# Filling the first operand tile of split queries and keys with GpSimd copies instead of DMA moves

## The chip, the cores and the metric

One core of a Trainium2 chip runs the kernel. The metric is the device time of one execution in microseconds, the median of three runs. Engines are TensorE (PE in the profile, its weight loads PEld), VectorE (DVE), ScalarE (ACT), GpSimd (POOL) and SyncE (SP, here the queue that issues nearly all DMAs of the stage in question; `SPq` in a row is the issue of a DMA on it).

## The reference

Three parts follow one another; the change lies in the first, attention with a causal mask and a bias from cumulated sums:

```python
def _attn_ref(q, k, v, s):          # q, k, v: (4, 8, 576, 64) float32
    scores = scale * np.matmul(q, k.transpose(0, 1, 3, 2))
    cum = np.cumsum(np.maximum(s, 0.0), axis=-1)
    bias = -(cum[:, :, :, None] - cum[:, :, None, :])
    scores = np.where(causal, -1e9, scores + np.minimum(bias, 0.0))
    scores = scores - np.max(scores, axis=-1, keepdims=True)
    attn = np.exp(scores)
    attn = attn / (np.sum(attn, axis=-1, keepdims=True) + 1e-09)
    return np.matmul(attn, v)
...
x = _moe_ref(x=x, ...)              # 2304 tokens, 8 experts of capacity 288, 512 -> 1024 -> 512
return _moe2_ref(x=x, ...)          # 512 -> 2048 -> 512 for all tokens
```

## The kernel before, in words

The 32 heads of attention are worked off in 8 groups `g` of 4 heads, and each group in two pairs `pr` of 2 heads. A head takes 7 steps ("blocks") of the main loop, so a group takes `NB` = 28. The loop at the end of `attention` runs over the step number `t`; in each step it calls what was put into `todo` for this step, emits the scores of one block (`emit_s`), one or two jobs, and five blocks later the product with V (`emit_pv`). The order on every engine is the order in which this loop emits; there is no planner behind it. `later(n, fn)` puts a function n steps ahead, `job(early, due, fn)` puts one into a list that is worked off when there is time.

Float32 products are made of split operands: a number is a high part (`float32r`) and a low part, the difference. For q and k that works so. `load_qk` (L728 to L737) loads a pair in six DMAs into `qkraw[pr]`, the last of which (n = 5, L736) is the end of k, 64 rows of two heads. `t_unit` (L836) transposes with TensorE in three units: L844 for most of it, L849 for the last 64 rows of q and k, which thus waits for that last load. Behind each unit `evac` (L855, ScalarE) writes the high part into a buffer `qk` of four planes, and `low` (L860, VectorE) the low part. There are two such buffers, so a pair's ScalarE write waits until the moves out of the buffer two pairs before are done.

`dup` (L871) then spreads a pair over the operand tiles of the scores: `QKA[i]` (i = g mod 2; partitions 0 to 63 hold the high parts of q and k, further rows the bias, which L868 and L869 bring) and `QKB[i]` (low and high parts on 64 partitions each). Per pair that is six moves, two into `QKA` (n = 0, 1, one per head) at once and four into `QKB` (n = 2 to 5) some steps later. One moves 64 partitions x 1152 columns, 288 KB. A string says how each one is made: `a` by ScalarE, `v` by VectorE, `d` by a DMA of the SP queue. In steady groups all six are `d`. `guard` (L920) computes from `QKA` the row maxima, `m_row` writes them back (L961), and `emit_s` multiplies both tiles (L999, L1001).

Behind the scores ScalarE makes `P` = exp (L1008), ScalarE (L1011) or VectorE (L1015) its high part `Ph`, and GpSimd the low part `Pl` = P - Ph (L1016). GpSimd does this once per tile of scores, four times a head, in the order of widths 384, 384, 320, 512. Three products with V follow (L1036, L1037, L1038), of which the last reads `Pl`. Beside this VectorE reduces the maxima (L937) and, from step 75 on, prepares weights of the last part in three instructions per unit (L115, L118, L121).

On the SP queue all loads (`qkraw`, `vraw`, weights), all `d` moves, the bias rows, the maxima and the stores of results (L1071, L1074) stand in one line, in the order of emission.

Of the kernel before, what the change touches and what calls it, by code (L numbers as in the profile page):

```python
# [9 lines left out]
F32R = mybir.dt.float32r  # L10
# [10 lines left out]
B, H, S, D = 4, 8, 576, 64  # L21
# [9 lines left out]
def fb(ap):  # L31
    return ap.bitcast(F32)
# [677 lines left out]
def attention(ctx, tc, const, cv, q, k, v, s, w_gate, ident, L, x_dram, b_dram, setup):  # L710
    nc = tc.nc
# [105 lines left out]
    def later(n, fn, *args):  # L817
        todo.setdefault(now[0] + n, []).append((fn, args))
# [3 lines left out]
    def job(early, due, fn, *args):  # L822
        jobs.append((due, len(jobs), early, fn, args))
        jobs.sort()
# [11 lines left out]
    def t_unit(g, pr, n):  # L836

        if n == 0:
            QK[g, pr] = rot.tile([128, 4, S], F32R, name="qk", bufs=2)
        st = QK[g, pr]  # L840
        p = bank()
        if n < 2:
            for r in range(4):
                nc.tensor.transpose(p[:, 128 * r:128 * r + 128], qkraw[pr][:, n, r], ident)  # L844
            src, hd = p, st[:, 1 + n, 0:512]
            los = [(src, hd, st[:, 3 * (1 - n), 0:512])]
        else:
            for t in range(2):
                nc.tensor.transpose(p[:, 128 * t:128 * t + 128], qkraw[pr][:, t, 4], ident)  # L849
            src = p[:, :256].rearrange("p (t c) -> p t c", t=2)[:, :, :64]  # L850
            hd = st[:, 1:3, 512:]
            los = [(src[:, t], st[:, 1 + t, 512:], st[:, 3 * (1 - t), 512:]) for t in range(2)]

        def evac():
            nc.scalar.activation(hd, src, AF.Copy)  # L855
            later((1, 4)[pr] if g == 0 else 0, low)

        def low():
            for x, h, ld in los:
                nc.vector.tensor_sub(ld, x, fb(h))  # L860
        later(1, evac)
        if n == 2:
            later(max(2, NB * g + 14 * pr - 41 - now[0]) if g or pr == 0 else 2, dup, g, pr)

    def bias_rows(g, pr):
        i, hs = g % 2, slice(2 * pr, 2 * pr + 2)
        rows = b_dram[4 * g + 2 * pr:4 * g + 2 * pr + 2].rearrange("h j t -> j h t")
        nc.sync.dma_start(out=fb(QA[i])[66:68, hs, 64:], in_=rows[0:2])  # L868
        nc.sync.dma_start(out=fb(KA[i])[64:66, hs], in_=rows[2:4])  # L869

    def dup(g, pr):  # L871
        i = g % 2
        if g:
            bias_rows(g, pr)
        st = fb(QK[g, pr])
        moves = []
        for dst, r, t in ((fb(QKA[i])[0:64, :, 64:], 0, 1), (fb(QKB[i])[0:64], 0, 2), (fb(QKB[i])[64:128], 1, 0)):
            for e in range(2):
                moves.append((dst[:, 2 * pr + e], st[64 * e:64 * e + 64, t:t + 2].rearrange("p t c -> p (t c)")))

        def move(n):
            dst, src = moves[n]
            how = ('vvaaaa', 'adaddd')[pr][n] if g == 0 else 'dddvda'[n] if g == 1 else "d"
            if how == "a":
                nc.scalar.activation(dst.bitcast(F32R), src, AF.Copy)
            elif how == "v":
                nc.vector.tensor_copy(dst.bitcast(F32R), src)
            else:
                nc.sync.dma_start(out=dst, in_=src)
        for n in range(len(moves)):  # L890
            if n < 2:
                move(n)
            else:
                later(2 * n - 2 if g > 1 else (2, 4)[pr] + (0, 0, 2, 4, 3, 5)[n], move, n)
        units = GU if g else GU0
        for u in range(len(units)):
            at = u + 2 if g == 0 and pr else now[0] + {0: 1, 1: 5}.get(g, 8) + u
            job(at, max(at, NB * g + 14 * pr - 26 + 2 * u), guard, g, pr, u)
# [234 lines left out]
    t = -PRE  # L1133
    while t < len(blocks) or queue or jobs or any(k >= t for k in todo):
# [14 lines left out]
        if 7 - PRE <= t < 15 - PRE:  # L1149
            x, h = divmod(t - 7 + PRE, 4)  # L1150
# [49 lines left out]
```

## Time and profile before

| what | value |
|---|---|
| median of 3 runs | 1037.19 us (1036.14 to 1038.14) |
| the profiled execution's own time | 1036.92 us |
| its span, first to last instruction | 1035.2 us |
| mean granted clock of TensorE over the span | 0.978 |
| TensorE busy | 959.4 us (93%) |
| VectorE, ScalarE, GpSimd busy | 604.1, 632.3, 424.0 us |
| DMA moved | 105.57 MB in 133298 packets |

The first 290 us or so are attention, the rest the experts and the last part. In a row of instructions stand the start and the length in us, the engine, the line, the operation, what it writes and reads, and how many are merged; in brackets the idle time of the engine before it and what ended that. A row of waits gives the sum in us, the number of waits and the longest. Granted clock 1.00 is full speed.

### The profile page before, as it was taken

How to read it: one execution, taken by the hardware profiler on the slowest of the kernel's cores; microseconds unless marked ns; L12 is line 12 of the kernel's file. 1: busy time of each engine (PE TensorE's matmuls, PEld its weight loads, DVE VectorE, ACT ScalarE, POOL GpSimd, SP SyncE). 2: the span in 40 equal slices, each digit the busy share in tenths (PEclk: the TensorE clock that was granted, in tenths of full speed). 3: DMA queues.
4: the chain of work that ended last, by engine and by line, in shares of the span. 5: the costliest groups of instructions: out<-in, count | busy, mean ns of one | idle time of the engine just before them, and what ended most of it. 6: DMA issues, size and time to landing. Idle time of an engine off the chain costs nothing.

```text
span 1035.2 us, 21414 instructions
## 1 busy us (share of the span) xinstructions
PE 959.4 (93%) x7679; PEld 905.8 (88%) x7679; DVE 604.1 (58%) x1871; ACT 632.3 (61%) x1403; POOL 424.0 (41%) x429
## 2 busy tenths in 40 slices
PE   5889889988978789899999999999999999999996
PEld 4779878888846678899999999999999999999996
DVE  6767889889576667546444553644644554343343
ACT  7657767766944356536745754673674575575573
POOL 2546666666768622360351234126036024502401
PEclk8889999999999999999999999999999999999999
DMA  5798889894229323231230222213123022401200
GB/s 125 178 189 203 202 205 212 203 215 127 73 85 285 106 79 112 76 106 42 64 100 9 82 67 62 65 42 105 42 65 105 19 67 83 136 12 31 76 1 23
DMA packets 133298, 105.57 MB, mean 102 GB/s; under 512 B 63720, under 2 KB 114056, under 8 KB 133160
## 3 DMA queue, kind: packets, MB, share of 16 engines
q1 hardware_dynamic: 122520, 83.50, 32.0%
q10 hardware_dynamic: 7600, 11.27, 3.6%
q0 software_dynamic: 3072, 9.44, 3.0%
q8 instruction: 60, 0.98, 0.4%
q14 instruction: 46, 0.38, 0.1%
HBM read 69.55 MB, written 9.73 MB: 77 GB/s over the span
## 4 chain that ended last, share of the span: by engine, by line
PE 57%; issue 13%; DVE 12%; ACT 6%; POOL 6%; DMA 4%; SPq 1%; ACTq 0%; POOLq 0%; DVEq 0%
PE y L497 8%; PE y L498 7%; PE y L499 7%; PE hp L497 5%; PE hp L498 5%; PE hp L499 5%; PE words L497 3%; PE words L499 2%; PE words L498 2%; PE rt L298 2%; DVE junk L937 2%; DMA QKB<-qk 2%; POOL WI L92 1%; PE t L1081 1%; POOL WO L92 1%
## 5 line engine op out<-in xcount | busy, mean ns | idle before, releaser
L467 POOL TENSOR_TENSOR wt<-raw,wt 128x512 fp32r<-128x512 f32 x112 | 142.9, 1292 | 195.0 <-ACT wt L466 193.9
L1016 POOL TENSOR_TENSOR Pl<-P,Ph 128x384 fp32r<-128x384 f32 (+2 forms) x128 | 136.7, 1076 | 92.6 <-DVE Ph L1015 45.8
L497 PE MATMUL y<-act,WO 128*128 128x288 f32 x516 | 154.9, 300 | 3.2 <-ACT act L558 3.2
L498 PE MATMUL y<-act,WO 128*128 128x288 f32 x516 | 153.7, 298 | 0.2
L499 PE MATMUL y<-act,WO 128*128 128x288 f32 x516 | 152.7, 296 | 0.0
L497 PE MATMUL hp<-xu,WI 128*128 128x288 f32 x372 | 114.4, 307 | 7.8 <-DVE c L599 3.9
L498 PE MATMUL hp<-xu,WI 128*128 128x288 f32 x372 | 110.2, 296 | 0.4 <-DVE xu L535 0.2
L499 PE MATMUL hp<-xu,WI 128*128 128x288 f32 x372 | 110.0, 296 | 0.0
L497 PEld LDWEIGHTS y<-act,WO 128*128 128x128 f32 x516 | 97.8, 190 | 3.5 <-ACT act L558 3.4
L498 PEld LDWEIGHTS y<-act,WO 128*128 128x128 f32 x516 | 97.6, 189 | 0.9 <-DVE act L605 0.6
L499 PEld LDWEIGHTS y<-act,WO 128*128 128x128 f32 x516 | 97.5, 189 | 0.0
L466 ACT ACTIVATE wt<-raw 128x512 fp32r<-128x512 f32 x112 | 70.1, 626 | 41.3 <-PE y L499 17.1
L402 POOL DMA_INDIRECT xg<-x_dram,idx x24 | 22.6, 942 | 162.2 <-DVE rt L408 156.9
L599 DVE SCALAR_TENSOR_TENSOR hp<-c,hp 128x288 f32<-128x288 f32 x75 | 34.6, 461 | 87.6 <-ACT c L594 87.6
L591 ACT ACTIVATE c<-c 128x288 f32<-128x288 f32 x128 | 56.3, 440 | 44.8 <-DVE c L590 41.7
L1008 ACT ACTIVATE P<-s 128x384 f32<-128x384 f32 (+2 forms) x128 | 63.5, 503 | 30.6 <-PE s L1001 17.6
L497 PEld LDWEIGHTS hp<-xu,WI 128*128 128x128 f32 x372 | 70.5, 190 | 11.8 <-DVE c L599 5.6
L1036 PE MATMUL pv<-Ph,VH 128*128 128x320 f32 (+4 forms) x224 | 71.8, 320 | 1.5 <-DVE xT L1055 1.5
L498 PEld LDWEIGHTS hp<-xu,WI 128*128 128x128 f32 x372 | 70.4, 189 | 1.0 <-DVE xu L579 0.6
L999 PE MATMUL s<-QKB 128*128 128x320 f32 (+4 forms) x224 | 70.4, 314 | 0.8 <-DVE mx L937 0.8
L499 PEld LDWEIGHTS hp<-xu,WI 128*128 128x128 f32 x372 | 70.5, 190 | 0.0
L497 PE MATMUL y<-act,wt 128*128 128x288 f32 x224 | 69.1, 309 | 0.0
(287 smaller groups left out, 2939.1 us busy)
## 6 DMA issues: line engine op xcount, KB each, us to landing
raw<-in_moe_w_dram SPq DMA_DIRECT2D x120, 256.0 KB
QKB<-qk SPq DMA_DIRECT2D x55, 288.0 KB
QKA<-qk SPq DMA_DIRECT2D x29, 288.0 KB
qkraw<-in_q_dram SPq DMA_DIRECT2D x32, 128.0 KB
qkraw<-in_k_dram SPq DMA_DIRECT2D x32, 128.0 KB
vraw<-in_v_dram SPq DMA_DIRECT2D x32, 128.0 KB
x_dram<-xn SPq DMA_DIRECT2D x16, 256.0 KB
r<-in_moe_w_in_dram ACTq DMA_DIRECT2D x8, 512.0 KB
```

The costliest lines, as they stand in the source:

```text
L402: nc.gpsimd.indirect_dma_start(out=xg[:JW], out_offset=None, in_=x_dram, in_offset=bass.IndirectOffsetOnAxis(ap=idx[:JW, j:j + 1], axis=0))
L466: nc.scalar.activation(t[:, 0], r, AF.Copy)
L467: nc.gpsimd.tensor_sub(t[:, 1], r, fb(t)[:, 0])
L497: nc.tensor.matmul(out_ap, ah, bh, start=first, stop=False)
L498: nc.tensor.matmul(out_ap, ah, bl, start=False, stop=False)
L499: nc.tensor.matmul(out_ap, al, bh, start=False, stop=last)
L591: nc.scalar.activation(a, a, AF.Exp)
L599: nc.vector.scalar_tensor_tensor(u, a, 0.5, p[:, :CAP], op0=OP.subtract, op1=OP.mult)
L999: nc.tensor.matmul(p[:m, at:at + n], KB[i][:, h, kc], QB[i][:, h, q0:q1], start=ti in (1, 2) and j == 0, stop=False, skip_group_check=True)
L1008: nc.scalar.activation(P[:, :n], p[:, :n], AF.Exp, scale=0.125)
L1016: nc.gpsimd.tensor_sub(Pl[:, :n], P[:, :n], fb(Ph)[:, :n])
L1036: nc.tensor.matmul(o, VH[i][:, a, hs], ph, start=first, stop=False)
```

## The change

In every group but the first, the moves n = 0 and 1 (into `QKA`) are no longer DMAs. Each is made by two GpSimd copies of 64 partitions x 576 columns, one for q and one for k, so four copies in a row per pair. And the four later moves, in groups from the third on, are emitted at 1, 3, 5 and 7 steps behind `dup` instead of 2, 4, 6 and 8.

```diff
         def move(n):
             dst, src = moves[n]
-            how = ('vvaaaa', 'adaddd')[pr][n] if g == 0 else 'dddvda'[n] if g == 1 else "d"
-            if how == "a":
+            how = ('vvaaaa', 'adaddd')[pr][n] if g == 0 else 'ppdvda'[n] if g == 1 else 'ppdddd'[n]
+            if how == "p":
+                for t in range(2):
+                    x = slice(S * t, S * t + S)
+                    nc.gpsimd.tensor_copy(dst.bitcast(F32R)[:, x], src[:, x])
+            elif how == "a":
                 nc.scalar.activation(dst.bitcast(F32R), src, AF.Copy)
...
             if n < 2:
                 move(n)
             else:
-                later(2 * n - 2 if g > 1 else (2, 4)[pr] + (0, 0, 2, 4, 3, 5)[n], move, n)
+                later(2 * n - 3 if g > 1 else (2, 4)[pr] + (0, 0, 2, 4, 3, 5)[n], move, n)
```

Below are places where the order on an engine changes; line numbers behind L884 are 4 higher in the changed kernel. First the SP queue of before at the second pair of the fifth group (`QKA_102` and `QKB_104` are that group's operand tiles, `qkraw_89` the raw tile of the pair after it):

```order
L961 DMA QKA_103<-mt 1x5x128 x2
L78 DMA r_2065<-in_moe_w_out_dram 128x256
L868 DMA QKA_102<-b_dram 2x2x576
L869 DMA QKA_102<-b_dram 2x2x576
L889 DMA QKA_102<-qk 64x1152 x2
L736 DMA qkraw_89<-in_k_dram 64x2x64
L889 DMA QKB_104<-qk 64x1152 x2
L733 DMA qkraw_90<-in_q_dram 128x4x64
```

And the SP queue of the change at the same place:

```order
L965 DMA QKA_103<-mt 1x5x128 x2
L78 DMA r_2079<-in_moe_w_out_dram 128x256
L868 DMA QKA_102<-b_dram 2x2x576
L869 DMA QKA_102<-b_dram 2x2x576
L736 DMA qkraw_89<-in_k_dram 64x2x64
L893 DMA QKB_104<-qk 64x1152 x2
L733 DMA qkraw_90<-in_q_dram 128x4x64
```

The two `QKA` moves are gone from between the bias rows and the last load of k; nothing else has changed its place here.

GpSimd before, around the same `dup`:

```order
L1016 TENSOR_TENSOR Pl<-P,Ph 128x384 x2
L1016 TENSOR_TENSOR Pl<-P,Ph 128x320
L1016 TENSOR_TENSOR Pl<-P,Ph 128x512
L1016 TENSOR_TENSOR Pl<-P,Ph 128x384 x2
L1016 TENSOR_TENSOR Pl<-P,Ph 128x320
```

GpSimd in the change:

```order
L1020 TENSOR_TENSOR Pl<-P,Ph 128x384 x2
L1020 TENSOR_TENSOR Pl<-P,Ph 128x320
L1020 TENSOR_TENSOR Pl<-P,Ph 128x512
L887 CAST QKA_102<-qk 64x576 x4
L1020 TENSOR_TENSOR Pl<-P,Ph 128x384 x2
L1020 TENSOR_TENSOR Pl<-P,Ph 128x320
```

The four copies stand between the last difference of one head, 512 wide, and the first of the next, 384 wide.

The third place is the SP queue in the start, where the first pair of the third group begins. Before (`QKA_102` and `QKB_104` are the third group's, `QKB_105` the second's):

```order
L889 DMA QKB_105<-qk 64x1152
L868 DMA QKA_102<-b_dram 2x2x576
L869 DMA QKA_102<-b_dram 2x2x576
L889 DMA QKA_102<-qk 64x1152 x2
L889 DMA QKB_105<-qk 64x1152
L733 DMA qkraw_89<-in_k_dram 128x4x64
L889 DMA QKB_104<-qk 64x1152
```

In the change:

```order
L893 DMA QKB_105<-qk 64x1152
L868 DMA QKA_102<-b_dram 2x2x576
L869 DMA QKA_102<-b_dram 2x2x576
L893 DMA QKB_105<-qk 64x1152
L893 DMA QKB_104<-qk 64x1152
L733 DMA qkraw_89<-in_k_dram 128x4x64
```

The last move of the second group has no `QKA` moves ahead of it any more, and the first `QKB` move of the third group now follows it directly, ahead of a load of k.

## Rows read from the trace of the kernel before

**Rows 1.** The page, parts 1 and 2: busy us, and tenths in 40 slices of the span

```profile
PE 959.4 (93%) x7679; PEld 905.8 (88%) x7679; DVE 604.1 (58%) x1871; ACT 632.3 (61%) x1403; POOL 424.0 (41%) x429
...
PEclk8889999999999999999999999999999999999999
DMA  5798889894229323231230222213123022401200
```

**Rows 2.** Busy time by stretch: window, length, engines (instructions), clock, DMA share, GB/s

```profile
22.00:68.00 46.00, 35.76 (x210) 32.13 (x211) 29.26 (x103) 27.62 (x54) 23.13 (x22) 0.76 0.87 185
68.00:156.00 88.00, 81.11 (x600) 74.80 (x600) 70.89 (x247) 62.43 (x141) 54.40 (x49) 0.98 0.86 198
156.00:235.00 79.00, 71.70 (x533) 64.67 (x531) 70.03 (x238) 57.18 (x128) 50.05 (x55) 1.00 0.90 210
```

**Rows 3.** Waits of TensorE, 68 to 235 us: sum, times, longest

```profile
PE t L849 <- DMA qkraw<-in_k_dram: 10.0, 7, 3.2
PE t L931 <- DVE mx L937: 1.5, 4, 0.5
```

**Rows 4.** Instructions in order of time on SP's queue, 135.6 to 137 us

```profile
135.67 1.18 SPq L889 DMA_DIRECT2D QKA<-qk  x2
136.90 0.99 SPq L736 DMA_DIRECT2D qkraw<-in_k_dram  x1
```

**Rows 5.** Instructions in order of time on TensorE, at 142.03 us

```profile
142.03 0.33 PE L849 MATMUL t<-ident,qkraw 128*128 128x128 f32 x1 [3.18 <-DMA qkraw<-in_k_dram]
```

**Rows 6.** Waits of TensorE, 22 to 68 us

```profile
PE t L849 <- issue: 3.2, 1, 3.2
PE t L931 <- DVE qk L860: 3.2, 1, 3.2
```

**Rows 7.** Waits of ScalarE, 22 to 68 us

```profile
ACT qk L855 <- DMA QKB<-qk: 6.6, 2, 3.9
```

**Rows 8.** The chain of waits, 40 to 66 us: start, length, what

```profile
44.11 3.55 DMA QKB<-qk
...
56.46 4.88 DMA QKB<-qk
```

**Rows 9.** Instructions in order of time on SP's queue, 35 to 36 and 55 us

```profile
35.30 1.11 SPq L889 DMA_DIRECT2D QKA<-qk  x2
...
55.07 1.29 SPq L889 DMA_DIRECT2D QKA<-qk  x2
```

**Rows 10.** Busy time by stretch, as rows 2, behind three long waits

```profile
48.00:54.00 6.00, 4.64 (x18) 3.93 (x19) 5.49 (x14) 2.83 (x7) 2.81 (x3) 0.50 0.88 175
62.00:68.00 6.00, 5.18 (x21) 4.84 (x22) 3.62 (x13) 2.56 (x7) 1.47 (x2) 0.50 1.17 205
143.00:147.00 4.00, 4.00 (x23) 4.00 (x21) 4.00 (x9) 1.60 (x5) 3.30 (x3) 0.57 1.06 250
```

**Rows 11.** The page, part 6: DMA issues, KB of one

```profile
QKA<-qk SPq DMA_DIRECT2D x29, 288.0 KB
```

**Rows 12.** Groups of instructions on GpSimd to 290 us: busy us, mean ns, idle before

```profile
L1016 POOL TENSOR_TENSOR Pl<-P,Ph 128x384 fp32r<-128x384 f32 x64 | 67.5, 1057 | 62.6 <-DVE Ph L1015 43.2 <-ACT Ph L1011 8.6 <-PE t L931 5.4
L1016 POOL TENSOR_TENSOR Pl<-P,Ph 128x512 fp32r<-128x512 f32 x32 | 41.8, 1307 | 21.7 <-ACT qk L855 9.1 <-ACT Ph L1011 5.6 <-PE t L931 5.5
...
L800 POOL TENSOR_SCALAR_AFFINE_SELECT band<-band 128x576 f32<-128x576 f32 x1 | 0.8, 763 | 0.1
...
L804 POOL COPY idwg<-ident 128x128 f32<-128x128 f32 x1 | 0.3, 287 | 0.0
```

**Rows 13.** Instructions in order of time on GpSimd, 201.4 to 204.5 us

```profile
201.52 1.28 POOL L1016 TENSOR_TENSOR Pl<-P,Ph 128x512 fp32r<-128x512 f32 x1 [1.08 <-ACT Ph L1011]
203.35 1.01 POOL L1016 TENSOR_TENSOR Pl<-P,Ph 128x384 fp32r<-128x384 f32 x1 [0.56 <-ACT Ph L1011]
```

**Rows 14.** Instructions in order of time on TensorE, at 206.14 us

```profile
206.14 0.28 PE L1038 MATMUL pv<-Pl,VH 128*128 128x256 f32 x1
```

**Rows 15.** Two lines of VectorE, 60 to 260 us: duration in ns, min/median/max

```profile
L1015 DVE CAST Ph<-P x48: 311/360/1002, 64.0 to 254.5; 128x384 fp32r<-128x384 f32 x24, 128x320 fp32r<-128x320 f32 x24
...
L115 DVE TENSOR_SCALAR xu<-r x9: 279/521/1269, 124.5 to 194.2; 128x256 int32<-128x256 int32 x9
```

## The prediction

> **What bounds the kernel now.** I read the page first: TensorE is busy for 959 of 1035 us, and its granted clock falls below full only in the first quarter; there, too, the 16 DMA engines are at 8 or 9 tenths, and in no later stretch of that length [rows 1]. So the stage to look at is attention, about 22 to 287 us, since the change touches nothing behind it. The stretches of that stage come next [rows 2]: from 68 to 235 us TensorE is busy 152.8 of 167 us, VectorE 140.9, GpSimd 104.5, DMA at 0.86 to 0.90; from 22 to 68 us TensorE is busy 35.8 of 46 at clock 0.76. TensorE is what sets the pace, and what is to be won is its idle time and its slow clock.
>
> The waits of TensorE between 68 and 235 us name one cause: L849, the last transposes of a pair, waited 10.0 us in seven places for the load of `qkraw` from k; the next group is 1.5 us [rows 3]. The SP queue around the longest of them shows why [rows 4]: the two `QKA` moves of the pair before (1.18 us of issue) stand directly ahead of the last k load, which is issued at 136.90 us though it is only 32 KB, and TensorE goes on at 142.03 us after 3.18 us of waiting [rows 5], 5.1 us after the issue. At the 198 GB/s of that stretch the two moves, 2 x 288 KB = 0.59 MB, fill the DMA engines for 3.0 us.
>
> In the start, 22 to 68 us, TensorE waited 3.2 us at L849 (its cause is not named, "issue") and 3.2 us at L931 [rows 6]; in the same stretch ScalarE's L855 waited 6.6 us in two places for a `QKB` move [rows 7], because it rewrites the `qk` buffer that the move still reads. The chain shows both: a `QKB` move issued at 44.11 us and landing 3.55 us later, and one at 56.46 us, 4.88 us, each followed by ScalarE, VectorE and TensorE [rows 8]. Both stand behind `QKA` moves on SP: a pair of 1.11 us at 35.30, and one of 1.29 us directly ahead at 55.07 [rows 9]; a third lies between.
>
> [...]
>
> **The change part by part.** Removed: 28 of the 29 `QKA<-qk` moves of 288 KB [rows 11] (7 groups x 2 pairs x 2 heads; the one left is the first group's). Each pair frees SP of some 1.2 us and the DMA engines of 3.0 us just ahead of the k load.
>
> *Steady part.* The k load is issued 1.2 us earlier and has 3.0 us less ahead of it, so it comes 4.2 us earlier, which is more than the longest of the seven waits. All 10.0 us go, with the 1.7 us of slow clock behind the longest: -11.7 us. What is late next there is VectorE, below.
>
> *Start.* The first `QKB` move has only one pair of moves ahead of it in SP's queue: 1.1 us earlier, so 3.2 becomes 2.1 us, and I let its slow clock stand: -1.1 us. The second has three pairs ahead: 3.5 us of issue, and 3.0 us less data in the engines, more than its wait; it goes with the 2.6 us of slow clock: -5.8 us. Sum -6.9 us. Bounds: only the issue time counts, -3.5; both waits and both clocks go, 3.2 + 3.2 + 2.3 + 2.6 = -11.3 us.
>
> *The `QKB` moves one block earlier.* They stay behind the k load on SP, and the heads that they overwrite were last read two blocks before. Cost nothing: if one had to wait on SP, the k load would already be out, and what is queued behind it are loads for a pair that is transposed a half group later. Without that cover it is one wait of L855 as in the start, 3.2 us at most.
>
> *Added on GpSimd:* 56 copies of 64x576, four in a row, in 14 places. The trace has no such copy. Nearest is the one-input `affine_select` of 128x576 at 763 ns; the only copy, 128x128, took 287 ns [rows 12]. Bounds: the copy's 287 ns in proportion to 576 columns, 1.29 us; half the two-input slope (1307 - 1057 ns over 128 columns, 1.95 ns a column), 0.56 us. I take 0.76, a burst of 3.05 us. No SP or DMA wait is behind it; queued behind it on GpSimd is the next `Pl` difference, and TensorE's third P x V product (L1038) waits for that. The room at such a place: `Pl` 512 ended at 202.80 us, the next one began 0.55 us later [rows 13] and ended at 204.36, and L1038 used it at 206.14 [rows 14]: 0.55 + 1.78 = 2.3 us. A burst of 3.05 exceeds that by 0.7 us. That place is among the tighter, so I take 0.4 us for each of the 11 places in the steady part: +4.4 us; in the start GpSimd is busy half the time [rows 2], nothing. Bounds: 0 at 0.56 us a copy; at 1.29 us a burst is 5.2 us, 2.9 too long, +31 us. [...]
>
> *VectorE.* The cast L1015 takes 311 ns at least and 1002 at most, L115 279 and 1269 [rows 15]; the excess, 0.7 and 1.0 us, is about one GpSimd instruction. So each burst may hold up two VectorE instructions by one copy: 1.5 us, 11 times 16 us. VectorE's idle time from 68 to 235 us is 167 - 140.9 = 26.1 us; with 11.7 us of the stretch gone 14.4 are left, less than 16. VectorE comes to its limit, and I give back +4 us; bounds 0 and, with all of the steady gain lost, +11.7. [...]
>
> The sum: -11.7 - 6.9 + 4.4 + 4.0 = -10.2 us. The profiled execution took 1036.92 us, 0.3 under the median of the runs, 1037.19. So 1027.0 us.
>
> **Rivals.** (1) *Everything goes and nothing comes back:* the copies fit into GpSimd's gaps (0.56 us) and VectorE keeps up. For it: GpSimd idles 37% of the steady part. Against: the room of 2.3 us and VectorE's load. -11.7 - 11.3 = -23.0: 1014 us.
> (2) *VectorE becomes the bound:* the waits at L849 turn into waits for L937 and L1096, and bursts cost their 4.4 us; only the start is won. For it: VectorE is busy 70.0 of 79 us from 156 to 235, TensorE 71.7. Against: 81% from 68 to 156 us, where the longest wait lies. -6.9 + 4.4: about 1034.5 us.
> (3) *Slower: the copy is long.* At 1.29 us the bursts cost 31 us at L1038: -18.6 + 4 + 31 = +16, about 1053 us. It decides from the point where 11 x (4X - 2.3) exceeds 14.6 us: X above 0.91 us. For it: the 287 ns of a small copy, if mostly columns; half the sources lie on other partitions than the targets, which no GpSimd row shows. Against: the 763 ns of 576 columns.
>
> **How the numbers follow.** Forecast 0.66, with its own range 1018 to 1033; rival 1 0.10; rival 2 0.12; rival 3 0.12. Under 0.2%, 2 us, this kernel's measurement can't tell from no change. Faster: 0.64 + 0.10 + 0.07 of rival 2 = 0.81; same: 0.02 + 0.04 = 0.06; slower: 0.12 + 0.01 = 0.13. The range 1014 to 1037 leaves out rival 3 and a little beyond rival 1.
>
> **What would show it.** Right: no wait of L849 for `qkraw` from k above 1 us; one low-clock stretch left in the start; copies near 0.76 us. Wrong: L1038 waiting for `Pl` by more than 10 us in sum; L849's wait still there (then the load's own travel was the cause); TensorE's idle time from 68 us on unchanged but under VectorE's name; copies over 0.91 us.

## The result, and the profile after

The changed kernel takes 1028.28 us (six runs, 1027.31 to 1029.18) against 1037.99 us for the kernel before on the same chip: ratio 0.9907, 95% interval 0.9894 to 0.9920, 9.7 us faster. Forecast were 10.2 us. The profiled execution took 1027.31 us, 9.6 us less than the one of before.

First the page of the kernel after, the rows that answer to [rows 1]: busy us by engine, and tenths in 40 slices of the span.

```profile
PE 957.2 (93%) x7679; PEld 901.2 (88%) x7679; DVE 607.1 (59%) x1871; ACT 631.8 (62%) x1403; POOL 462.1 (45%) x485
...
PEclk8999999999999899999999999999999999999998
DMA  5677686763147423231231121213123122401200
```

GpSimd is busy 38 us more, with 56 instructions more; the DMA digits of the attention stage have fallen from 8 and 9 to 6 and 7, and the clock's digits of 8 in the first quarter are gone, but for the very first. By stretch, as in [rows 2] (window, length, engines, clock, DMA share, GB/s):

```profile
22.00:68.00 46.00, 38.12 (x259) 34.06 (x260) 34.84 (x126) 31.97 (x65) 35.24 (x39) 0.91 0.68 158
68.00:156.00 88.00, 83.79 (x626) 76.58 (x624) 73.58 (x252) 65.62 (x148) 71.70 (x73) 1.00 0.77 181
156.00:235.00 79.00, 71.74 (x516) 63.21 (x515) 72.40 (x233) 54.75 (x122) 64.23 (x76) 1.00 0.68 166
```

DMA is relieved everywhere, and the start runs at clock 0.91 instead of 0.76. But in the third row TensorE is no busier than before (71.7 us) although nothing waits for a load any more; VectorE is busy for 72.4 of 79 us, more than TensorE. The waits of TensorE from 68 to 235 us, the answer to [rows 3] (sum, times, longest):

```profile
PE t L935 <- ACT xn L1102: 3.1, 6, 0.7
PE pv L1040 <- DVE xT L1059: 2.3, 3, 1.5
PE t L935 <- DVE mx L941: 2.2, 5, 0.8
PE pv L1042 <- POOL Pl L1020: 1.5, 5, 0.5
PE t L957 <- DVE mx L941: 1.0, 1, 1.0
```

The 10.0 us at L849 are gone to the last of the seven. In their place stand many small waits for VectorE, directly or over ScalarE's evacuation L1102, which itself waits for a VectorE addition (L1100, 17.4 us in sum). And the start, the answer to [rows 6] and [rows 7] (two answers, TensorE's and ScalarE's waits from 22 to 68 us):

```profile
PE t L935 <- DVE mx L941: 3.3, 4, 1.3
PE t L849 <- issue: 1.4, 1, 1.4
```

```profile
ACT qk L855 <- DMA QKB<-qk: 2.2, 1, 2.2
```

One of the two long waits is left, with 1.4 us instead of 3.2; the other is gone with its `QKB` move; the waits for VectorE's L941 are longer (3.3 us, 0.8 at the same line, L937, before).

TensorE's instructions stand in the same order in all kernels here, so the same one can be sought in each. The last product with V begins at 287.33 us before and 279.33 after:

```profile
287.33 0.31 PE L1038 MATMUL pv<-Pl,VH 128*128 128x320 f32 x1
```

```profile
279.33 0.31 PE L1042 MATMUL pv<-Pl,VH 128*128 128x320 f32 x1
```

So attention accounts for 8.0 us of the profiles' 9.6. The first such product of head 4, behind the start, comes at 76.17 before and 69.74 after, 6.4 us earlier: 6.4 us are won in the start and 1.6 in the steady part, which here and below means the stretch from head 4 to that last product. The last 1.6 us lie behind attention, where nothing was changed; they are scatter between executions (the first experiment below ends attention 0.07 us before the kernel before and its span is still 1.8 us shorter).

How busy the engines are in this same stretch of work, the kernel before and then the change (columns as in [rows 2], two answers):

```profile
76.17:287.33 211.16, 192.83 (x1433) 176.27 (x1431) 172.12 (x563) 154.97 (x347) 139.13 (x134) 0.99 0.75 177
```

```profile
69.74:279.33 209.59, 194.75 (x1430) 176.03 (x1431) 173.72 (x562) 154.45 (x346) 167.32 (x175) 1.00 0.62 150
```

VectorE's busy time rises by 1.6 us only, so the copies do not load it much beyond what it had; TensorE idles 3.5 us less and is busy 1.9 us longer.

The copies on GpSimd and two lines of VectorE (min/median/max in ns; copies over the whole span, VectorE from 60 to 260 us, as in [rows 15]; the last row is L121 in the kernel before; four answers):

```profile
L887 POOL CAST QKA<-qk x56: 652/664/1195, 34.0 to 228.5; 64x576 fp32r<-64x576 f32 x56
```

```profile
L1019 DVE CAST Ph<-P x51: 311/425/1157, 59.8 to 257.9; 128x320 fp32r<-128x320 f32 x26, 128x384 fp32r<-128x384 f32 x25
```

```profile
L121 DVE SCALAR_TENSOR_TENSOR xu<-r,xu x9: 415/1115/1658, 119.7 to 187.2; 128x256 int32<-128x256 int32 x9
```

```profile
L121 DVE SCALAR_TENSOR_TENSOR xu<-r,xu x9: 413/426/1665, 126.9 to 195.4; 128x256 int32<-128x256 int32 x9
```

The copies take less than the 0.76 us assumed. The median of the casts grew from 360 to 425 ns, that of L121 from 426 to 1115; by the mean L121 grew from 849 to 995 ns, and L115, the other line of [rows 15], fell from 745 to 639.

### The profile page after: what moved, and what is told of

The parts are those of the page before. It is cut to its first block, busy times and chain, and to the rows that moved or that the text cites. A ratio compares the mean times of both kernels' runs of the same rounds, so it can differ in the third digit from the quotient of the medians.

```text
span 1025.6 us, 21405 instructions
## 1 busy us (share of the span) xinstructions
PE 957.2 (93%) x7679; PEld 901.2 (88%) x7679; DVE 607.1 (59%) x1871; ACT 631.8 (62%) x1403; POOL 462.1 (45%) x485
## 4 chain that ended last, share of the span: by engine, by line
PE 60%; DVE 14%; issue 13%; ACT 6%; POOL 5%; DMA 1%; ACTq 0%; SPq 0%; POOLq 0%; DVEq 0%
PE y L497 8%; PE y L498 7%; PE y L499 7%; PE hp L497 5%; PE hp L498 5%; PE hp L499 5%; PE words L497 3%; PE words L499 2%; PE words L498 2%; PE rt L298 2%; PE t L935 2%; PE pv L1042 1%; PE pv L1040 1%; DVE junk L941 1%; PE s L1005 1%
```

## The experiments

They ran in three sets, each with its own runs of the kernel before, so ratios are compared. The changed kernel itself was not run again in them; its ratio was 0.9907, and experiment 2, which ends attention at the same time, has 0.9932 on another chip, so differences of some 2.5 us between sets say nothing. "Attention ends" is the start of that last product with V in the run's profile, "head 4" that of the first such product of head 4; both are read from one profile of each kernel.

**1 and 2. The earlier `QKB` moves alone, and the change without them.**

```diff
# 1, in the kernel before
-                later(2 * n - 2 if g > 1 else ...
+                later(2 * n - 3 if g > 1 else ...
# 2, in the changed kernel
-                later(2 * n - 3 if g > 1 else ...
+                later(2 * n - 2 if g > 1 else ...
```

> The kernel before with only the four QKB moves emitted one step earlier in groups from the third on; all six moves stay DMAs. If the gain of 9.7 us is that of the missing QKA moves, this is within 1.5 us of the kernel before (ratio 0.999 to 1.001). If the earlier QKB moves have a share in it, 2 to 4 us faster; if they crowd the DMA engines ahead of the k load, 2 us or more slower.

> The changed kernel with the QKB moves put back to 2, 4, 6 and 8 steps behind dup. If the shift costs and brings nothing: 1028 us, ratio 0.990 to 0.992. If the shift is part of the gain: 1030 to 1032 us. The two runs on the shift should agree in sign.

Measured: alone 1.0003 (0.9993 to 1.0014), attention ends at 287.26; without them 0.9932 (0.9918 to 0.9947), attention ends at 279.41. The shift does nothing; the gain is that of the first two moves.

**3. Neither the `QKA` moves nor the copies.**

```diff
             if how == "p":
+                if g > 1: return
```

> The changed kernel without the GpSimd copies from the third group on (the operand tile's first rows keep what the group two before left there, so these parts of the scores are those of other heads): neither the QKA moves nor the copies are there. Theory V (VectorE takes over as the bound in the steady part, whatever GpSimd does): attention ends at most 2 us earlier than in the changed kernel, 1026 to 1028 us. Theory G (the copies give back what the DMAs bring, by delaying Pl and by holding up VectorE through blocked casts): 6 to 9 us faster than the changed kernel, 1019 to 1022 us, and the casts of L1019 back to the durations of the kernel before.

Measured: 0.9872 (0.9855 to 0.9890); attention ends at 276.32, 11.0 us before the kernel before, 3.0 before the changed one. By the medians of the same set it is 5.6 us faster than experiment 2 (1022.82 against 1028.41 us); the profile shows less mostly because its start is 1.7 us later, partly at clock 0.57 (last section). From head 4 (71.47) on it needs 204.85 us, the kernel before 211.16, the changed one 209.59. So in the steady part the missing moves are worth 6.3 us, and the copies take back 4.7. Neither theory alone is right. TensorE's waits from 68 to 235 us without the copies:

```profile
PE t L937 <- ACT xn L1104: 3.6, 7, 0.7
PE t L937 <- DVE mx L943: 2.8, 6, 0.8
PE pv L1042 <- DVE xT L1061: 1.2, 2, 1.0
...
PE pv L1044 <- POOL Pl L1022: 0.2, 1, 0.2
```

VectorE's waits are there without any copy. L121, now without copies beside it, is back at its durations in the kernel before (median 425, mean 847 ns), and in the steady part VectorE is busy 170.3 instead of 173.7 us (two answers):

```profile
L121 DVE SCALAR_TENSOR_TENSOR xu<-r,xu x9: 411/425/1655, 120.8 to 185.9; 128x256 int32<-128x256 int32 x9
```

```profile
71.47:276.32 204.85, 192.47 (x1433) 175.60 (x1432) 170.26 (x563) 154.27 (x347) 138.91 (x134) 1.00 0.62 152
```

So the copies lengthen VectorE's instructions by some 3.5 us in sum, and TensorE's waits for `Pl` by 1.3 (from 68 to 235 us). That the 3.5 us are the rest of the 4.7 fits in size; it is not shown wait by wait.

**4. The copies in addition to the DMA moves.**

```diff
+            if n < 2 and g:
+                for t in range(2):
+                    x = slice(S * t, S * t + S)
+                    nc.gpsimd.tensor_copy(spare, src[:, x])
```

> The kernel before with all its DMA moves and, in addition, the 56 copies on GpSimd at the places of the change, into a spare bf16 tile that nobody reads. It measures the copies by themselves. Theory V: 0 to 2 us slower than before (1038 to 1040). Theory G: 4 to 9 us slower (1042 to 1047), with L1038 waiting for Pl or VectorE's casts longer; waits at L849 partly hide this, so the lower half is likelier.

Measured: 1.0043 (1.0017 to 1.0069); attention ends at 290.84, 3.5 us later. But one stretch alone holds more than that, TensorE at clock 0.50 for 9 us, where the kernel before is at 1.00:

```profile
184.00:193.00 9.00, 9.00 (x40) 8.57 (x40) 7.33 (x29) 4.19 (x10) 7.94 (x15) 0.50 1.00 221
```

By that clock half of the 9 us, 4.5, is my estimate of what the stretch cost, more than the 3.5, so this profile shows no price of the copies. The ratio does, though: by the medians the run is 3.2 us slower, and the clock doesn't explain that, since its nine executions have the same mean granted clock as those of the kernel before, 0.976. TensorE's waits from 68 to 235 us (the load was 10.0 us before):

```profile
PE t L850 <- DMA qkraw<-in_k_dram: 3.6, 3, 2.4
PE t L936 <- ACT xn L1103: 3.0, 6, 0.7
PE pv L1043 <- POOL Pl L1021: 1.8, 6, 0.5
```

New waits stand where waits for the load of k were. The price of a copy thus can't be read from a kernel that still waits; 3.2 us lies between the two theories, and the run doesn't tell them apart.

**5. The copies one per step.**

```diff
+                    for t in range(2):
+                        later((0, 2)[n] + t, part, n, t)   # part: one copy
```

> The changed kernel with the four copies of a pair, from the third group on, one per step (0, 1, 2, 3 behind dup) instead of four in a row. The copies cost some 4.7 us of the steady part (attention ends 11.0 us before that of the kernel before without them, 8.0 with them). If they cost it as a burst in front of Pl: L1042's wait for Pl (1.5 us) goes and attention ends 2 to 4 us earlier than in the changed kernel, 1024 to 1026 us. If they cost it by holding up VectorE one instruction at a time: no change or 1 us slower, 1028 to 1029 us.

Measured: 0.9952 (0.9933 to 0.9970), attention ends at 281.95. Slower than the change, though TensorE's wait for `Pl` from 60 to 240 us is 0.2 instead of 1.5 us. From head 4 (72.52) on it needs 209.43 us, like the changed kernel's 209.59; the loss is in the start, where TensorE's clock is 0.79 from 48 to 56 us. Taking the wait for `Pl` away brought the steady part nothing, so the burst was not what held it.

**6 and 7. The cast of the second tile on ScalarE, in the changed kernel and in the one before.**

```diff
-            on_act = ti in (0,3)
+            on_act = ti in (0, 1, 3)
```

> The changed kernel with the high part of P of the second score tile made by ScalarE's exponential instead of VectorE's cast: 32 casts of 128x384 less on VectorE, some 14 us, and 32 activations of about 0.48 us more on ScalarE. Theory V (VectorE is the bound of the steady part): attention ends 3 to 6 us earlier, 1022 to 1025 us, and TensorE's waits for L941, L1059 and L1102 shrink. Rival (it is only the chain of small waits, with ScalarE in it): no gain, or 1 to 3 us slower, with P (L1012) later.

> The same edit of the casts in the kernel before. Theory V: before, the load of k sets the pace of the steady part and VectorE lies under its waits, so the edit brings little here: 0 to 2 us faster, waits at L849 still 8 us or more. Rival (VectorE's lag cost the kernel before as much): as much faster as in the changed kernel, 3 us or more.

Measured: 0.9919 (0.9902 to 0.9936) and attention's end at 279.21 in the changed kernel; 1.0007 (0.9993 to 1.0021) and 285.89 in the one before. No gain, a miss. The edit hardly lightens VectorE: with 22 casts gone from 60 to 240 us, VectorE is busy 153.6 instead of 155.2 us, and the casts that stay, 128x320, take 764 ns on the mean instead of 535. In the steady part, 14.4 us of casts gone lower its busy time by 3.7 us only; 7.5 us come back in the other casts.

**8. The copies on ScalarE.**

```diff
-... else 'ppdddd'[n]
+... else 'aadddd'[n]
```

> The changed kernel with the copies of the third and later groups on ScalarE, two of 64x1152 per pair, some 1.16 us each as L889 takes, 24 of them, 28 us in all, and none on GpSimd. If GpSimd's copies cost through GpSimd (burst or blocked casts): casts of VectorE as short as in the kernel before, and attention ends 0 to 3 us earlier than in the changed kernel. If any engine's copy costs as much because it stands in front of the chain P, Ph, Pl: ScalarE delays P by 2.3 us per pair and it is 2 to 8 us slower than the changed kernel, 1030 to 1036 us. I take the second for likelier.

Measured: 0.9956 (0.9940 to 0.9972), attention ends at 283.35, 4.0 us later than with GpSimd, as expected; 1.8 of them lie in the start, 2.2 in the steady part. GpSimd is the better place. That the casts would be as short as before was wrong: those of 128x384 take 604 ns on the mean (398 before, 510 in the changed kernel). So a cast grows longer with no copy on GpSimd beside it; why, no run shows.

**9 and 10. VectorE lightened, in the changed kernel and in the one before.** These leave out L118 and L121 of the weight preparation in attention.

```diff
-                nc.vector.scalar_tensor_tensor(b, ...)
+                if not keep:
+                    nc.vector.scalar_tensor_tensor(b, ...)
... (the same for the second)
```

> The changed kernel without the second and third VectorE instruction (L118, L121) of each weight preparation that falls into attention, some 25 us of VectorE from 60 to 240 us (those weights are then not the right ones; the work behind attention is the same). Theory V: the small waits for L941, L1059 and, over the evacuations of the 't' banks, L1102 (9 us together in the changed kernel) halve, and attention ends 3 to 6 us earlier, 11 to 14 us before that of the kernel before. Rival (GpSimd's burst and the products with V hold TensorE): less than 1 us. Moving casts to ScalarE brought nothing, but took only 1.6 us from VectorE, since the other casts grew from 0.54 to 0.76 us.

> The same two instructions left out in the kernel before. Theory V: there the waits for the k load stay and hide VectorE, so 0 to 2 us; the change is then worth 11 to 14 us with VectorE lightened, against 8.0 without. Rival: as much as in the changed kernel, so the change is worth the same.

Measured: 0.9828 (0.9813 to 0.9842), attention ends at 268.57, in the changed kernel; 0.9978 (0.9966 to 0.9990) and 284.51 in the one before. The same edit is worth 10.8 us behind the change and 2.8 without it, and the change is worth 15.9 us of attention with a light VectorE (16.2 by the medians) and 8.0 with the real one. TensorE's waits from 68 to 235 us, changed kernel first:

```profile
PE pv L1044 <- POOL Pl L1022: 5.9, 13, 1.3
PE pv L1042 <- DVE xT L1061: 1.8, 2, 1.4
PE t L937 <- DVE mt L963: 0.5, 1, 0.5
PE t L937 <- DVE mx L943: 0.4, 1, 0.4
```

```profile
PE t L851 <- DMA qkraw<-in_k_dram: 11.8, 6, 3.1
PE t L933 <- DVE mx L939: 0.8, 2, 0.5
```

In the changed kernel the waits over L1102 are gone and those for L941 nearly so, and now, not earlier, TensorE waits for `Pl`, the burst's wait. GpSimd, too, is busy less in the steady part (163.3 instead of 167.3 us), but TensorE's waits for it grow, so the gain doesn't come from there. In the kernel before, TensorE comes to the load of k earlier and waits longer, 11.8 instead of 10.0 us. Part of its small gain went to the clock, 0.94 and 0.96 in the two long stretches instead of 0.98 and 1.00, so 2.8 us is on the low side:

```profile
68.00:156.00 88.00, 82.05 (x595) 77.04 (x595) 66.61 (x240) 61.94 (x140) 53.63 (x48) 0.94 0.85 197
156.00:235.00 79.00, 71.46 (x529) 66.56 (x527) 60.52 (x219) 57.16 (x127) 48.65 (x55) 0.96 0.90 210
```

**11 and 12. The copies two steps later, and that with the first long move on GpSimd.**

```diff
# 11, in the changed kernel
+                if g > 1:
+                    later(2, move, n)
# 12, as 11 and
-... 'ppdvda'[n] if g == 1
+... 'ppdvpa'[n] if g == 1
```

> The changed kernel with the four copies, from the third group on, two steps later: behind the first Pl of a head, where GpSimd idles 2.0 us, instead of ahead of it, where it idles 0.55. If Pl held up by the burst is what the copies cost: L1042's wait for Pl goes (1.5 us), attention ends 1 to 3 us earlier, 1025 to 1027 us. If it is blocked casts of VectorE (the cast of the second tile falls into the same gap): no gain or 1 to 2 us slower.

> As the run with later copies, and in addition the move n = 4 of the second group on GpSimd instead of by DMA: the DMA of 3.5 us for which ScalarE's L855 and over it L849 waits in the start. The 1.4 us wait at 46 us goes; and since behind that same wait the clock fell in three of the runs and not in three others (48 to 56 us at 0.57 to 0.67 or at 1.00, some 2 us), it should not fall there: 1 to 2 us faster than the run with later copies. Rival: four more copies hold up Pl in the start by as much: no difference.

Measured: 0.9958 (0.9944 to 0.9972), attention ends at 282.41; and 0.9947 (0.9932 to 0.9962), 279.23. The first is a miss: the wait for `Pl` fell to 0.2 us, and VectorE's waits grew, now with L860 among them (2.4 us in six waits from 60 to 240 us); why L860 comes later stays open. The second part does what was expected: the wait at 46 us is gone, head 4 comes at 67.98 instead of 69.53, and attention ends 3.2 us earlier than with the later copies alone. By the medians that is 1.4 us, and the intervals overlap. Neither beats the change. The move on GpSimd without the later copies, and a VectorE that really has less to do with all of its results right, were not run.

## Why the prediction was right, step by step

- **The waits at L849, -11.7 us: right.** All seven went, and the slow clock behind the longest too (0.57 before [rows 10], 1.00 from 68 us on now). No run shows the 1.7 us of slow clock in this term, nor the 2.6 and 2.3 us in the start's, as times of their own: they are estimates, the busy times of [rows 10] times what the clock there, 0.57 and 0.50, lacks of 1.00. At the place of the longest, the load was issued 1.7 us ahead of the first of the two transposes before (136.90 and 138.57 us) and is issued 3.5 us ahead now:

```profile
138.57 0.27 PE L849 MATMUL t<-ident,qkraw 128*128 128x128 f32 x1
```

```profile
127.94 0.70 SPq L736 DMA_DIRECT2D qkraw<-in_k_dram  x1
...
131.47 0.38 PE L849 MATMUL t<-ident,qkraw 128*128 128x128 f32 x2
```

  The earlier issue alone, 1.9 us, would not do for a wait of 3.2; the load also takes less time than before, at most some 3.6 us from issue to use instead of 5.1. Both parts of the working are borne out. That the gain of this term was the full 11.7 us can't be read off, since the waits of the next engine set in at once.
- **The start, -6.9 us: right in sum (-6.4), not in its parts.** The first wait fell to 1.4 us, not 2.1, and its slow clock, which I let stand (0.50 from 48 to 54 us [rows 10]), went in this profile (1.00 from 34 to 68 us), though not in all kernels with the same wait (last section); the second went as forecast. New waits for L941, 3.3 instead of 0.8 us, took 2.5 back.
- **The earlier `QKB` moves, 0: right,** by experiments 1 and 2.
- **The copies, 0.76 us and +4.4: the size was off.** A copy takes 0.66 us at the median and 0.72 on the mean, and TensorE's wait for `Pl` is 1.5 us in all, in five places. At the place of [rows 13] the four take 2.87 us, and L1042 waits 0.50 us:

```profile
194.54 2.87 POOL L887 CAST QKA<-qk 64x576 fp32r<-64x576 f32 x4
197.49 1.06 POOL L1020 TENSOR_TENSOR Pl<-P,Ph 128x384 fp32r<-128x384 f32 x1
```

```profile
198.61 0.38 PE L1042 MATMUL pv<-Pl,VH 128*128 128x256 f32 x1 [0.50 <-POOL Pl L1020]
```

  2.87 less the room of 2.3 us is 0.57, as the working has it; other places had more room than the 0.4 us taken for each allowed. Experiment 9 shows what that room was: with a light VectorE the wait is 5.9 us. TensorE came late to those places for another reason, so that `Pl` was ready.
- **VectorE, +4.0 us: the right engine, the reason mostly wrong, and too small.** The steady part won 1.6 us instead of 11.7 - 8.4 = 3.3, so 10.1 us came back. In the steady part TensorE's listed waits for anything but loads rose from 7.8 to 14.5 us: 1.5 of the 6.7 are for `Pl`, 5.2 for VectorE, directly or over L1102. The remaining 3.4 us stand in no wait; TensorE's busy time rose by 1.9 us although its clock is no longer low (1.00, 0.99 before). That they are VectorE's too is argued from experiment 9, where busy time falls to 188.3 us.

  The working expected bursts to hold up VectorE by 16 us, an estimate from the durations of [rows 15]. VectorE's busy time says otherwise: the copies add 3.5 us to it (experiment 3). And 5.4 us (11.7 - 6.3) come back in experiment 3, which has no copy there: TensorE, once it no longer waits for loads, catches up with a VectorE that is nine tenths busy (72.6 of 79 us). Only 4.7 come back with the copies, the waits for `Pl` among them. Experiment 9 is the test: with VectorE lightened the steady part takes 198.80 us, 12.4 less than before. The bound that I gave, +11.7, holds the term.
- **The sum is better than its parts, and that is luck.** Of the two give-backs one was too high and the other too low. Attention's own 8.0 us stand against the forecast 10.2, and 1.6 of the 9.6 us in the profiles are scatter behind attention. On the chip of experiment 2, whose attention ends 0.08 us behind the change's, the gain is 7.1 us.
- **Rivals.** Rival 1, nothing comes back, is what a light VectorE comes near to: 15.9 of its 23.0 us. Rival 2 named the right next bound; it had the start right (-6.9, measured -6.4), but the steady part won 1.6 us where it lost 4.4 at the bursts, whose wait was 1.5 us. Rival 3 fell with the copy's 0.66 us.

## What to carry to other kernels

A wait that goes is worth what the next engine leaves of it (here 10.0 us of waits went and the steady part won 1.6): before costing it, look at the busy share of every engine that feeds the same stage, in that stage, and ask which one is within a few per cent of the waiting one; here 70.0 beside 71.7 us said it. To measure such a hidden second limit, lighten it in both kernels; here its price showed nearly only in the one without the wait (10.8 against 2.8 us). And a cheap transfer behind large ones in one queue, here 32 KB behind 590, can be the one that all wait for (10.0 us of TensorE's waits).

## What the runs showed of the hardware that was not expected

The clock of TensorE doesn't fall behind a wait of a given length every time. At 46 us the change and experiments 2, 6 and 9 have the same wait at L849 as experiments 3, 5 and 8 (1.2 to 1.5 us); the granted clock stays at 1.00 in the first four and falls in the other three. The changed kernel and experiment 3, 48 to 56 us:

```profile
48.00:56.00 8.00, 5.91 (x41) 5.13 (x41) 7.87 (x28) 5.00 (x10) 7.24 (x8) 1.00 0.79 182
```

```profile
48.00:56.00 8.00, 7.57 (x33) 6.96 (x33) 7.82 (x26) 3.58 (x9) 5.98 (x5) 0.57 0.76 168
```

Head 4 is 1.7 us later in the second, and experiment 4 lost 4.5 us in such a stretch. Differences of 2 to 4 us between single profiles of these kernels may be nothing else. The split is not one of chance alone, it seems: the four that stay at 1.00 have the copies at the same places, the three that fall have them elsewhere or not at all, and come out of the wait 0.4 to 0.8 us later (47.9 to 48.3 us, against 47.5 in the change). What decides it stays open; no run was made for it, and each kernel has one profile.

Moving half of VectorE's casts away shortened VectorE's load little (3.7 of 14.4 us in experiment 6), since the casts that were left took longer (535 to 764 ns on the mean). What makes them longer, no run shows.
